# Turned scores in a ring of four unit places, and the token MLP by halves of the channels

## The chip, the core and the metric

The kernel runs on one core of one Trainium2 chip. The metric is the device time of one execution in microseconds (us). Times are medians of several runs; a profile is one further execution, recorded by the hardware profiler, and its rows are what the working below is made of.

The engines of the core have these names in the profile: PE is the matrix engine, PEld its weight loads, DVE the vector engine, ACT the scalar engine, POOL the general one, SP the engine that here only issues DMAs. An engine works through its own instructions in the order in which they were written. "ACTq" and "SPq" rows are DMA issues.

## The reference, cut to what matters

All data are float32. There are 8 batches, 8 heads, 576 tokens, a head dimension of 64, 512 channels, a token MLP of width 256 and a channel MLP of width 1536.

```python
scores = q @ k.T / 8                                   # per batch and head, 576 x 576
thresh = scores.max(-1) - tau
scores = where(scores >= thresh, scores, -1e9)
attn = exp(scores - scores.max(-1)); attn /= attn.sum(-1) + 1e-9
x = heads_side_by_side(attn @ v)                       # batch x 576 x 512
u = x + (relu(x.T @ w_tok1) @ w_tok2).T                # token MLP, mixes tokens
out = u + relu(u @ w_ch1) @ w_ch2                      # channel MLP, mixes channels
```

## The kernel before, in words

**Units, visits, groups.** Attention is cut into 144 units of 128 rows of queries for two heads (a "pair" of heads). Nine units make a visit (two pairs of one batch; the middle unit, t = 4, is shared by both pairs), two visits make a batch. Units are numbered u = 0 to 143; the first batch is u = 0 to 17. Three units in a row (GU = 3) make a group, so a visit has groups 0, 1 and 2, and in a group the units have places 0, 1 and 2.

**One unit.** `scores` (L290s to L313): PE writes q k into two PSUM tiles (L306, pool of two, so a unit's tiles must be read before the next unit's scores), DVE takes the row maximum (L311), POOL makes a bias (L312). `weigh` (L315): ACT reads the scores (L321) into e, 128 x 1152, and takes the exponential with its row sum (L328). `norm` (L332): DVE takes reciprocals (L335, L336), POOL multiplies (L339).

**Turning e.** The product with v needs e with the keys on the partitions. In the first batch `turn` does that on PE (L357) with copies into a tile eT of a group (L359). In all later batches `turn_blocks` (L361) does it for the unit two before the running one: DVE transposes 32 x 32 blocks of e into a tile T of the group (L369), and after the third unit SP issues 16 DMAs (L378) that put the blocks where they belong in eT. T comes from a pool of two tiles with room for three units each; eT is a single tile. `values` (L395) multiplies eT with v on PE (L413, L418), two units after the group's last turn, and ACT copies the result into xT (L423).

```python
T = Ts[key]          # work.tile([P, 4, GU, NK * 32], tag="T"), one per group, two in turn
for a in range(4):
    for i in range(4):
        nc.sync.dma_start(out=eT[32 * a : 32 * a + 32, :, i, :], in_=T[32 * i : 32 * i + 32, a, :, :])
```

**MLPs as filling.** When a batch's values are done, `push` (L603) queues its token MLP, then its channel MLP, as small steps with costs, in `todo`; `fill` (L590) pops steps between the parts of later units, up to a quota. Old channel-MLP steps that are left over (about 45 us of them) are dealt out one ahead of every token step, and two ahead of the steps whose places `push` gets as `waits`. So the order in which PE works is written by this dealing.

`token_mlp` (L430) for a batch: 5 steps transpose xT on PE (L449), and ACT copies into x_sb (L450); 2 steps `tok1`, each 5 matmuls of 512 columns (L456), with a Relu on ACT into a tile `a` (L458); 8 steps `tok2`, each 2 matmuls of 288 columns (L466) and an addition into xT on DVE (L470). The first batch does this in two halves of the channels already, later batches at full width. A float32 matmul stands in the profile as two rows. tok1, tok2 and the channel MLP (`channel_mlp` L484; L509 with a Relu at L510, L530 with an addition at L542) take turns at two PSUM tiles, tag "mm"; each must be emptied by ACT or DVE before it is filled again.

**Loads.** v of a pair is loaded on SP (`load_v`, L110) into a pool of four tiles: at t = 3 of a visit the first pair of the next visit, at t = 7 its second pair (L730). SP's queue holds, in the order written, these loads, the 16 DMAs of each group, 16 small moves per channel-MLP block (L499) and the stores of the output (L549, L569).

Of the kernel before, what the change touches and what calls it, by code (L numbers as in the profile page):

```python
# [9 lines left out]
F32 = mybir.dt.float32  # L10
# [3 lines left out]
AF = mybir.ActivationFunctionType  # L14
ALU = mybir.AluOpType
AX = mybir.AxisListType

P = 128
# [3 lines left out]
def kernel(  # L22
# [25 lines left out]
    nc = tc.nc  # L48
    B, H, S, D = q.shape
    DM = H * D  # L50
# [3 lines left out]
    NI = 4  # L54
    MAIN = NI * P
    LAST = S - MAIN
    NT = NI + 1
    MT = [P] * NI + [LAST]
    NP = H // 2
    NTK = DTOK // P  # L60
    NCC = DM // P
    NJ = DCH // P
    HS = S // 2
    NK = 2 * S // P
# [3 lines left out]
    const = ctx.enter_context(tc.tile_pool(name="const", bufs=1))  # L68
    ld = ctx.enter_context(tc.tile_pool(name="ld", bufs=2))
    work = ctx.enter_context(tc.tile_pool(name="work", bufs=2))  # L70
# [3 lines left out]


    late = ctx.enter_context(ExitStack())
    ps_3rd = late.enter_context(tc.tile_pool(name="ps_3rd", bufs=1, space=bass.MemoryType.PSUM))
    ps_mm = None

# [2 lines left out]
    pairs = [(b, p) for b in range(B) for p in range(NP)]  # L82
# [27 lines left out]
    def load_v(n):  # L110

        b, p = pairs[n]
        lv = ld.tile([P, NK, D], F32, tag="lv", bufs=4, name=f"lv_{n}")
        nc.sync.dma_start(out=lv, in_=v[b].rearrange("h s d -> (h s) d")[2 * S * p : 2 * S * p + 2 * S, :].rearrange("(c p) d -> p c d", p=P))
        vals[n] = lv

# [14 lines left out]
    w1 = const.tile([P, NT, DTOK], F32, name="w1")  # L131
    w2 = const.tile([P, NTK, S], F32, name="w2")
    wc1 = const.tile([P, NJ, NCC, P], F32, name="wc1")
    wc2 = const.tile([P, NJ, DM], F32, name="wc2")

    x_sb = const.tile([P, NT, DM], F32, name="x_sb")
    nc.gpsimd.memset(x_sb[LAST:P, NI, :], 0.0)
    nc.gpsimd.memset(w1[LAST:P, NI, :], 0.0)

# [111 lines left out]
    def need(i):  # L251

        weight(3 * i + 4 - steps_done)

    load_piece(0)
    load_v(0)
    for i in range(1, NRAW):
        load_piece(i)
    load_v(1)


# [14 lines left out]
    st = {}  # L276
    xTs = {}
    eTs = {}
    Ts = {}

    def in_blocks(b):
        return b > 0
# [59 lines left out]
    GU = 3  # L342

    def turn(u, third):

        b, p0, t = units[u]
        key, place = (b, p0, t // GU), t % GU
        e = st[u]

        if third == 0 and place == 0:  # L350
            eTs[key] = work.tile([P, NK, GU * P], F32, tag="T", name=f"eT_{u}")
        if third == 2:
            st.pop(u)
        ps = ps_tr.tile([P, MAIN], F32, tag="tr", name=f"tr{third}_{u}")[:, 0 : 3 * P].rearrange("p (c x) -> p c x", c=3)
        for c in range(3):
            k0 = (3 * third + c) * P
            nc.tensor.transpose(out=ps[:, c, :], in_=e[:, k0 : k0 + P], identity=ident)  # L357
        on = nc.scalar.copy if third == 1 else nc.vector.tensor_copy
        on(out=eTs[key][:, 3 * third : 3 * third + 3, P * place : P * place + P], in_=ps)  # L359

    def turn_blocks(u):  # L361

        b, p0, t = units[u]
        key, place = (b, p0, t // GU), t % GU
        e = st.pop(u)
        if place == 0:
            Ts[key] = work.tile([P, 4, GU, NK * 32], F32, tag="T", name=f"T_{u}")
        T = Ts[key]
        nc.vector.transpose(  # L369
            out=T[:, :, place, :].rearrange("p a (c x) -> p c a x", c=NK), in_=e.rearrange("p (c a x) -> p c a x", c=NK, a=4)  # L370
        )
        if place == GU - 1:
            del Ts[key]
            eT = work.tile([P, GU, 4, NK * 32], F32, tag="eT", bufs=1, name=f"eT_{u}")
            eTs[key] = eT.rearrange("p n i (c x) -> p (n i) c x", c=NK)
            for a in range(4):
                for i in range(4):
                    nc.sync.dma_start(out=eT[32 * a : 32 * a + 32, :, i, :], in_=T[32 * i : 32 * i + 32, a, :, :])  # L378

    def split_middle(n):  # L380

# [8 lines left out]
    copies = deque()  # L390
# [34 lines left out]
                copies.append(lambda x=x, ps=ps: nc.vector.tensor_copy(out=x, in_=ps))  # L425


    hidden = {}

    def token_mlp(b, ps=range(NP)):  # L430

        xT = xTs[b]
        o = S * (b % 2)
        L = len(ps)
        cols = slice(P * ps[0], P * ps[0] + P * L)
        if b not in hidden:
            hidden[b] = work.tile([P, NTK, DM], F32, tag="a", bufs=1, name=f"a_{b}")
        a = hidden[b]

        def psum(name):  # L440
            return (ps_mm or ps_tr).tile([P, DM], F32, tag="mm" if ps_mm else "tr", name=name)

        def turn_x(t, n):
            M = MT[t]
            to = ps_tr.tile([P, MAIN], F32, tag="tr", name=f"tx_{b}_{t}_{ps[0]}")[0:M, 0 : n * L * P].rearrange("p (t c x) -> p t c x", t=n, c=L)
            for i in range(n):
                for c in range(L):
                    tok = o + (t + i) * P
                    nc.tensor.transpose(out=to[:, i, c, :], in_=xT[:, ps[c], tok : tok + M], identity=ident)  # L449
            nc.scalar.copy(out=x_sb[0:M, t : t + n, cols], in_=to.rearrange("q t p d -> q t (p d)"))  # L450

        def tok1(m):
            need(2)
            to = psum(f"t1_{b}_{m}_{ps[0]}")[:, 0 : P * L]
            for t in range(NT):
                nc.tensor.matmul(to, lhsT=w1[:, t, P * m : P * m + P], rhs=x_sb[:, t, cols], start=(t == 0), stop=(t == NT - 1))  # L456
            if ps_mm:
                nc.scalar.activation(out=a[:, m, cols], in_=to, func=AF.Relu)  # L458
            else:
                copies.append(lambda: nc.vector.tensor_scalar(out=a[:, m, cols], in0=to, scalar1=0.0, scalar2=None, op0=ALU.max))  # L460

        def tok2(c, f):
            need(6)
            to = psum(f"t2_{b}_{c}_{f}")[:, 0:HS]
            for m in range(NTK):
                nc.tensor.matmul(  # L466
                    to, lhsT=a[:, m, P * c : P * c + P], rhs=w2[:, m, HS * f : HS * f + HS], start=(m == 0), stop=(m == NTK - 1)
                )
            u = xT[:, c, o + HS * f : o + HS * f + HS]
            nc.vector.tensor_add(out=u, in0=u, in1=to)  # L470

        n = NI // L
        steps = [(0.11 * n * L, lambda t=t: turn_x(t, n)) for t in range(0, NI, n)] + [(0.11 * L, lambda: turn_x(NI, 1))]
        first = len(steps)
        steps += [(1.1 * L, lambda m=m: tok1(m)) for m in range(NTK)]
        steps += [(0.97, lambda c=c, f=f: tok2(c, f)) for c in ps for f in range(2)]
        return steps, (first, first + NTK)

# [120 lines left out]
    early = deque()  # L601

    def push(b):  # L603
        nonlocal quota
        uT = xTs[b]
        steps, waits = token_mlp(b) if b else token_mlp(b, range(NP // 2, NP))
        old = list(todo)
        todo.clear()
        todo.extend(early)
        early.clear()  # L610

        for i, step in enumerate(steps):
            n = 2 if i in waits else 1
            todo.extend(old[:n] + [step])
            del old[:n]
        todo.extend(old)
        for i in range(2) if b % 2 == 0 else range(2, (2 * S + GR - 1) // GR):
            todo.extend(channel_mlp(b - b % 2, uT, i))
        quota = (sum(c for c, _ in todo) - (KEEP if b else KEEP_FIRST)) / (UB - 1)
# [28 lines left out]
    for u in range(len(units) + LAG + 4):  # L648
        on = u < len(units)
        if u == UB:  # L650
            late.close()
            ps_mm = ctx.enter_context(tc.tile_pool(name="ps_mm", bufs=2, space=bass.MemoryType.PSUM))
        if on:
            b_now, p0, t = units[u]
            n = b_now * NP + p0
        w = u - LAG
        back = 0 <= w < len(units)
# [26 lines left out]
        while copies:  # L684
            copies.popleft()()
        if last and u < UB:
            early.extend(token_mlp(0, range(NP // 2))[0])
        elif last:
            push(0)
        if back:  # L690
# [11 lines left out]
        if back and in_blocks(wb):  # L702
            turn_blocks(w)
# [15 lines left out]
        if on:  # L719


            when = {3: (2, 0, 2), 4: (2, 2, 4), 5: (2, 4, 6), 6: (2, 6, 8), 8: (3, 0, 3), 0: (1, 3, 6), 1: (1, 6, 8)}
            if u == 0:
                load_qk(1, (nc.sync, nc.sync), range(0, 3))
            if t in when:
                m, lo, hi = when[t]
                if n + m < len(pairs):
                    load_qk(n + m, (nc.scalar if b_now else nc.sync,) * 2, range(lo, hi))
            if t in (3, 7) and n + 2 + t // 4 < len(pairs):
                load_v(n + 2 + t // 4)  # L730
            if t == 2:
                prep(n + 1)
            if t == 7 and n + 2 < len(pairs):
                prep(n + 2)
# [36 lines left out]
```

## Time and profile before

| what | value |
|---|---|
| median of 3 runs | 1352.67 us (1351.88 to 1352.94) |
| span of the profiled execution, first to last instruction | 1349.9 us |
| PE busy | 1306.6 us, 97% of the span |
| DVE busy | 592.2 us, 44% |
| ACT busy | 585.1 us, 43% |
| POOL busy | 352.5 us, 26% |
| DMA, mean rate | 100 GB/s |
| block transposes on DVE (L369) | 126 of 1364 ns |
| DMAs from T to eT (L378) | 672 of 108 KB, median 2.3 us from issue to landing |

The time that the profiled execution has outside its span isn't in the profile; its span is 2.8 us less than the median of the runs. A row of instruction groups gives line, engine, operation, tiles, shape and count, then after the bar busy time in us, mean ns of one, and the engine's idle time before them with what ended it. A timeline row gives start and length in us, and in brackets the idle time before it and what ended it. "PEclk" is the share of PE's full clock that was granted.

### The profile page before, as it was taken

How to read it: one execution, taken by the hardware profiler on the slowest of the kernel's cores; microseconds unless marked ns; L12 is line 12 of the kernel's file. 1: busy time of each engine (PE TensorE's matmuls, PEld its weight loads, DVE VectorE, ACT ScalarE, POOL GpSimd, SP SyncE). 2: the span in 40 equal slices, each digit the busy share in tenths (PEclk: the TensorE clock that was granted, in tenths of full speed). 3: DMA queues.
4: the chain of work that ended last, by engine and by line, in shares of the span. 5: the costliest groups of instructions: out<-in, count | busy, mean ns of one | idle time of the engine just before them, and what ended most of it. 6: DMA issues, size and time to landing. Idle time of an engine off the chain costs nothing.

```text
span 1349.9 us, 17890 instructions
## 1 busy us (share of the span) xinstructions
PE 1306.6 (97%) x6186; PEld 817.1 (61%) x6186; DVE 592.2 (44%) x1026; ACT 585.1 (43%) x1299; POOL 352.5 (26%) x683
## 2 busy tenths in 40 slices
PE   7888899999999999999999999999999999999999
PEld 5565556547474666655665567565656566575677
DVE  6878874445443435434334445434443454201000
ACT  6777654444445435443434444354333454120110
POOL 4565652222222213222222222222221222100000
PEclk8998999999999999999999999999999999999999
DMA  5535764535353544543345435535443453400000
GB/s 123 120 87 127 199 168 97 127 94 136 83 133 89 114 109 96 126 109 88 86 107 125 98 85 123 125 82 115 109 102 83 114 118 79 112 22 17 23 24 32
DMA packets 296746, 135.31 MB, mean 100 GB/s; under 512 B 204816, under 2 KB 289552, under 8 KB 296656
## 3 DMA queue, kind: packets, MB, share of 16 engines
q1 hardware_dynamic: 168944, 118.27, 34.4%
q10 hardware_dynamic: 127712, 15.90, 7.4%
q8 instruction: 49, 0.80, 0.3%
q14 instruction: 41, 0.34, 0.1%
HBM read 43.25 MB, written 9.44 MB: 39 GB/s over the span
## 4 chain that ended last, share of the span: by engine, by line
PE 86%; DVE 6%; DMA 3%; ACT 2%; SPq 1%; issue 1%; POOL 1%; ACTq 0%; DVEq 0%; POOLq 0%
PE c L530 26%; PE c L509 26%; PE sc L306 11%; PE pv L418 9%; PE t L456 5%; PE t L466 4%; PE pv L413 3%; DVE mx L311 2%; PE tx L449 1%; DMA lk<-in_k_dram 1%; ACT e L321 1%; SPq L378 1%; PE c_h L557 1%; DVE T L369 1%; DVE high L211 1%
## 5 line engine op out<-in xcount | busy, mean ns | idle before, releaser
L509 PE MATMUL c<-xT,wc 128*128 128x256 f32 (+1 forms) x1920 | 400.1, 362 | 0.1
L311 DVE TENSOR_REDUCE mx<-sc 128x1 f32<-128x576 f32 x288 | 204.4, 750 | 444.3 <-PE sc L306 443.2
L530 PE MATMUL c<-wc,g 128*128 128x512 f32 x840 | 379.0, 597 | 0.0
L509 PEld LDWEIGHTS c<-xT,wc 128*128 128x128 f32 x1920 | 334.9, 191 | 69.3 <-issue 29.7
L312 POOL TENSOR_SCALAR bias<-mx,toff 128x1 f32<-128x1 f32 x288 | 81.1, 282 | 775.6 <-DVE mx L311 722.7
L321 ACT ACTIVATE e<-sc,bias 128x576 f32<-128x576 f32 x288 | 199.8, 739 | 182.5 <-POOL bias L312 176.7
L530 PEld LDWEIGHTS c<-wc,g 128*128 128x128 f32 x840 | 154.7, 190 | 176.1 <-issue 172.4
L328 ACT ACTIVATE e<-e,ntau 128x576 f32<-128x576 f32 x288 | 221.1, 771 | 0.0
L339 POOL TENSOR_SCALAR e<-e,rr 128x576 f32<-128x576 f32 x288 | 214.3, 756 | 14.8 <-ACT g L510 2.6
L510 ACT ACTIVATE g<-c 128x256 f32<-128x256 f32 (+1 forms) x240 | 86.7, 361 | 296.5 <-PE c L509 283.4
L306 PE MATMUL sc<-kT,qT 64*128 64x288 f32 (+1 forms) x1280 | 190.3, 433 | 6.9 <-ACT e L321 5.9
L369 DVE STREAM_TRANSPOSE T<-e 128x1152 f32<-128x1152 f32 x126 | 171.9, 1364 | 5.5 <-DMA eT<-T 2.9
L306 PEld LDWEIGHTS sc<-kT,qT 64*128 64x128 f32 (+1 forms) x1280 | 105.2, 178 | 92.2 <-issue 57.2
L418 PE MATMUL pv<-eT,lv 128*64 128x384 f32 (+1 forms) x1024 | 136.8, 408 | 0.0
L418 PEld LDWEIGHTS pv<-eT,lv 128*64 128x64 f32 x1024 | 76.9, 138 | 49.9 <-issue 42.1
L423 ACT COPY xT<-pv 128x384 f32<-128x384 f32 (+1 forms) x56 | 21.0, 400 | 164.6 <-PE pv L418 159.5
L466 PE MATMUL t<-w,a 128*128 128x288 f32 x256 | 75.2, 421 | 8.2 <-DVE xT L470 4.8
L542 DVE TENSOR_TENSOR us<-c,ut 128x512 f32<-128x512 f32 x26 | 17.9, 690 | 137.5 <-PE c L530 122.7
L456 PE MATMUL t<-x_sb,w 128*128 128x512 f32 (+1 forms) x180 | 72.4, 549 | 0.0
L466 PEld LDWEIGHTS t<-w,a 128*128 128x128 f32 x256 | 45.9, 192 | 30.2 <-issue 10.5
L470 DVE TENSOR_TENSOR xT<-xT,t 128x288 f32<-128x288 f32 x64 | 28.3, 446 | 70.6 <-PE t L466 69.9
L328 ACT ACTIVATION_READ_ACCUMULATOR e<-e,ntau 128x1 f32 x288 | 56.7, 197 | 0.0
(51 smaller groups left out, 571.2 us busy)
## 6 DMA issues: line engine op xcount, KB each, us to landing
eT<-T SPq DMA_DIRECT2D x672, 108.0 KB, 2.3
scratch<-in_moe_w_ch_dram SPq DMA_DIRECT2D x24, 512.0 KB, 3.7
lv<-in_v_dram SPq DMA_DIRECT2D x32, 288.0 KB, 3.5
out_dram<-us SPq DMA_DIRECT2D x35, 256.0 KB, 2.2
lk<-in_k_dram ACTq DMA_DIRECT2D x109, 72.0 KB, 2.7
lq<-in_q_dram ACTq DMA_DIRECT2D x106, 72.0 KB, 2.3
ut<-us SPq DMA_DIRECT2D x192, 32.0 KB, 1.9
lk<-in_k_dram SPq DMA_DIRECT2D x19, 72.0 KB, 3.2
```

The lines of the kernel that those rows point to most:

```text
L306: nc.tensor.matmul(sc[h][rows, f, 0:HS], lhsT=qT[r, cols], rhs=kT[r, HS * f : HS * f + HS], start=True, stop=True)
L311: nc.vector.tensor_reduce(out=mx[:, c], in_=sc[h][:, :, 0:HS], axis=AX.XY, op=ALU.max)
L321: nc.scalar.activation(out=eh, in_=sc[h][:, :, 0:HS], func=AF.Prelu, bias=bias[:, h : h + 1], scale=SCALE, alpha=STEEP)
L328: nc.scalar.activation(out=eh, in_=eh, func=AF.Exp, bias=ntau, accum_out=rs[:, h : h + 1])
L339: nc.gpsimd.tensor_scalar(out=eh, in0=eh, scalar1=rr[:, h : h + 1], scalar2=1.0, op0=ALU.mult, op1=ALU.mult)
L369: nc.vector.transpose(out=T[:, :, place, :].rearrange("p a (c x) -> p c a x", c=NK), in_=e.rearrange("p (c a x) -> p c a x", c=NK, a=4))
L418: nc.tensor.matmul(to[r], lhsT=lv[:, j, :], rhs=e[j], start=False, stop=(c == NI - 1), skip_group_check=True)
L456: nc.tensor.matmul(to, lhsT=w1[:, t, P * m : P * m + P], rhs=x_sb[:, t, cols], start=(t == 0), stop=(t == NT - 1))
L466: nc.tensor.matmul(to, lhsT=a[:, m, P * c : P * c + P], rhs=w2[:, m, HS * f : HS * f + HS], start=(m == 0), stop=(m == NTK - 1))
L509: nc.tensor.matmul(ps, lhsT=wc1[:, j, c, :], rhs=uT[:, c, GR * i : GR * i + n], start=(c == 0), stop=(c == NCC - 1))
L510: nc.scalar.activation(out=s["g"][:, j, 0:n], in_=ps, func=AF.Relu)
L530: nc.tensor.matmul(flat, lhsT=s["g"][:, j, P * t : P * t + P], rhs=wc2[:, j, :], start=(j == 0 and b > 0), stop=(j == NJ - 1), skip_group_ ...
```

## The change

The tile T becomes one ring of four unit places (GU + 1). Groups with an even number fill places 0, 1, 2 and groups with an odd number fill 3, 2, 1; so the first unit of a group goes into the one place that the group before it did not use, and the second and third go into places that the group before it did use. The DMAs read the places in the order of the units. The ring's memory is taken when the first batch is over; until then a pool `first` holds there one of the two eT tiles of the first batch, and the other is the eT tile that later batches use.

The token MLP is cut into two halves of the channels for every batch. x_sb and `a` are half as wide, one of each, and used by both halves in turn. `token_steps` writes the new order: turns, tok1 of the first half; turns of the second half; tok2 of the first half; tok1, tok2 of the second half. That makes 18 steps in place of 15 and three places with two old steps ahead in place of two. v has three tiles in place of four: at t = 2 of a visit its own second pair is loaded, at t = 5 the first pair of the next visit.

```diff
+    first = late.enter_context(tc.tile_pool(name="first", bufs=1))
-        lv = ld.tile([P, NK, D], F32, tag="lv", bufs=4, name=f"lv_{n}")
+        lv = ld.tile([P, NK, D], F32, tag="lv", bufs=3, name=f"lv_{n}")
-    x_sb = const.tile([P, NT, DM], F32, name="x_sb")
+    x_sb = const.tile([P, NT, DM // 2], F32, name="x_sb")
...
-            eTs[key] = work.tile([P, NK, GU * P], F32, tag="T", name=f"eT_{u}")
+            odd = (u // GU) % 2
+            pool = work if odd else first
+            eTs[key] = pool.tile([P, NK, GU * P], F32, tag="eT", bufs=1, name=f"eT_{u}")
...
-        if place == 0:
-            Ts[key] = work.tile([P, 4, GU, NK * 32], F32, tag="T", name=f"T_{u}")
-        T = Ts[key]
+        back = (u // GU) % 2
+        slot = GU - place if back else place
         nc.vector.transpose(
-            out=T[:, :, place, :].rearrange("p a (c x) -> p c a x", c=NK), ...
+            out=T[:, slot].rearrange("p a (c x) -> p c a x", c=NK), ...
...
+            slots = slice(GU, 0, -1) if back else slice(0, GU)
-                    nc.sync.dma_start(..., in_=T[32 * i : 32 * i + 32, a, :, :])
+                    nc.sync.dma_start(..., in_=T[32 * i : 32 * i + 32, slots, a, :])
...
-        if b not in hidden:
-            hidden[b] = work.tile([P, NTK, DM], F32, tag="a", bufs=1, name=f"a_{b}")
-        a = hidden[b]
+        xs = slice(0, P * L)
+        a = work.tile([P, NTK, P * L], F32, tag="a", bufs=1, name=f"a_{b}_{ps[0]}")
...
+    def token_steps(b):
+        half = NP // 2
+        ta, ma, sa = token_mlp(b, range(half))
+        tb, mb, sb = token_mlp(b, range(half, NP))
+        n = len(ta) + NTK + len(tb)
+        return ta + ma + tb + sa + mb + sb, (len(ta), n, n + len(sa) + NTK)
...
-        steps, waits = token_mlp(b) if b else token_mlp(b, range(NP // 2, NP))
+        if b:
+            steps, waits = token_steps(b)
+        else:
+            turns, t1, t2 = token_mlp(b, range(NP // 2, NP))
+            steps, waits = turns + t1 + t2, (len(turns), len(turns) + NTK)
...
         if u == UB:
             late.close()
+            ring = ctx.enter_context(tc.tile_pool(name="ring", bufs=1))
+            T = ring.tile([P, GU + 1, 4, NK * 32], F32, name="T")
...
-            if t in (3, 7) and n + 2 + t // 4 < len(pairs):
-                load_v(n + 2 + t // 4)
+            if t in (2, 5) and 1 < n + 1 + t // 3 < len(pairs):
+                load_v(n + 1 + t // 3)
```

More of the change, by code (lines that the diff above doesn't have):

```diff
@@ L76 @@
     late = ctx.enter_context(ExitStack())
+    first = late.enter_context(tc.tile_pool(name="first", bufs=1))
+    T = None
     ps_3rd = late.enter_context(tc.tile_pool(name="ps_3rd", bufs=1, space=bass.MemoryType.PSUM))
@@ L278 @@
     eTs = {}
-    Ts = {}
     def in_blocks(b):
@@ L365, in turn_blocks @@
         e = st.pop(u)
-        if place == 0:
-            Ts[key] = work.tile([P, 4, GU, NK * 32], F32, tag="T", name=f"T_{u}")
-        T = Ts[key]
+        back = (u // GU) % 2
+        slot = GU - place if back else place
         nc.vector.transpose(
-            out=T[:, :, place, :].rearrange("p a (c x) -> p c a x", c=NK), in_=e.rearrange("p (c a x) -> p c a x", c=NK, a=4)
+            out=T[:, slot].rearrange("p a (c x) -> p c a x", c=NK), in_=e.rearrange("p (c a x) -> p c a x", c=NK, a=4)
         )
         if place == GU - 1:
-            del Ts[key]
             eT = work.tile([P, GU, 4, NK * 32], F32, tag="eT", bufs=1, name=f"eT_{u}")
             eTs[key] = eT.rearrange("p n i (c x) -> p (n i) c x", c=NK)
+            slots = slice(GU, 0, -1) if back else slice(0, GU)
             for a in range(4):
                 for i in range(4):
-                    nc.sync.dma_start(out=eT[32 * a : 32 * a + 32, :, i, :], in_=T[32 * i : 32 * i + 32, a, :, :])
+                    nc.sync.dma_start(out=eT[32 * a : 32 * a + 32, :, i, :], in_=T[32 * i : 32 * i + 32, slots, a, :])
     def split_middle(n):
@@ L425, in values @@
                 copies.append(lambda x=x, ps=ps: nc.vector.tensor_copy(out=x, in_=ps))
-    hidden = {}
     def token_mlp(b, ps=range(NP)):
@@ L434, in token_mlp @@
         L = len(ps)
-        cols = slice(P * ps[0], P * ps[0] + P * L)
-        if b not in hidden:
-            hidden[b] = work.tile([P, NTK, DM], F32, tag="a", bufs=1, name=f"a_{b}")
-        a = hidden[b]
+        xs = slice(0, P * L)
+        a = work.tile([P, NTK, P * L], F32, tag="a", bufs=1, name=f"a_{b}_{ps[0]}")
         def psum(name):
@@ L449, in turn_x @@
                     nc.tensor.transpose(out=to[:, i, c, :], in_=xT[:, ps[c], tok : tok + M], identity=ident)
-            nc.scalar.copy(out=x_sb[0:M, t : t + n, cols], in_=to.rearrange("q t p d -> q t (p d)"))
+            nc.scalar.copy(out=x_sb[0:M, t : t + n, xs], in_=to.rearrange("q t p d -> q t (p d)"))
         def tok1(m):
@@ L455, in tok1 @@
             for t in range(NT):
-                nc.tensor.matmul(to, lhsT=w1[:, t, P * m : P * m + P], rhs=x_sb[:, t, cols], start=(t == 0), stop=(t == NT - 1))
+                nc.tensor.matmul(to, lhsT=w1[:, t, P * m : P * m + P], rhs=x_sb[:, t, xs], start=(t == 0), stop=(t == NT - 1))
             if ps_mm:
-                nc.scalar.activation(out=a[:, m, cols], in_=to, func=AF.Relu)
+                nc.scalar.activation(out=a[:, m, :], in_=to, func=AF.Relu)
             else:
-                copies.append(lambda: nc.vector.tensor_scalar(out=a[:, m, cols], in0=to, scalar1=0.0, scalar2=None, op0=ALU.max))
+                copies.append(lambda: nc.vector.tensor_scalar(out=a[:, m, :], in0=to, scalar1=0.0, scalar2=None, op0=ALU.max))
         def tok2(c, f):
@@ L466, in tok2 @@
                 nc.tensor.matmul(
-                    to, lhsT=a[:, m, P * c : P * c + P], rhs=w2[:, m, HS * f : HS * f + HS], start=(m == 0), stop=(m == NTK - 1)
+                    to, lhsT=a[:, m, P * (c - ps[0]) : P * (c - ps[0]) + P], rhs=w2[:, m, HS * f : HS * f + HS], start=(m == 0), stop=(m == NTK - 1)
                 )
@@ L472, in token_mlp @@
         n = NI // L
[L473 to L477, printed above, removed]
+        turns = [(0.11 * n * L, lambda t=t: turn_x(t, n)) for t in range(0, NI, n)] + [(0.11 * L, lambda: turn_x(NI, 1))]
+        return turns, [(1.1 * L, lambda m=m: tok1(m)) for m in range(NTK)], [(0.97, lambda c=c, f=f: tok2(c, f)) for c in ps for f in range(2)]
+    def token_steps(b):
[4 more added lines that the diff above has]
+        return ta + ma + tb + sa + mb + sb, (len(ta), n, n + len(sa) + NTK)
     moves = deque()
@@ L686 @@
         if last and u < UB:
-            early.extend(token_mlp(0, range(NP // 2))[0])
+            early.extend(sum(token_mlp(0, range(NP // 2)), []))
         elif last:
```

## The prediction

> **What bounds the kernel now.** I read the page first, for the busy shares and the chain, then what PE waits for, then the timeline around single units.
>
> ```profile
> span 1349.9 us, 17890 instructions
> PE 1306.6 (97%) x6186; PEld 817.1 (61%) x6186; DVE 592.2 (44%) x1026; ACT 585.1 (43%) x1299; POOL 352.5 (26%) x683
> PE 86%; DVE 6%; DMA 3%; ACT 2%; SPq 1%; issue 1%; POOL 1%; ACTq 0%; DVEq 0%; POOLq 0%
> ```
>
> PE is busy for 97% of the span and carries 86% of the chain that ended last. By stretches (the windows view) its idle time lies before 310 us and in the last stores; from 310 to 1242 us it is 4.4 us. So there is little to gain: work taken off DVE, ACT or SP gives nothing, and whatever makes PE wait is added in full. What PE waits for in the token MLP, the part that the change rearranges:
>
> ```profile
> PE t L466 <- DVE xT L470: 4.8, 3, 3.0
> PE t L466 <- ACT g L510: 3.2, 3, 1.6
> PE tx L449 <- ACT x_sb L450: 1.7, 3, 1.2
> ```
>
> The columns are total us, times, longest. Together 9.7 us; without the 3.0 in the first batch, 6.7.
>
> **The ring's wait.** In the built program of the changed kernel, the second turn of every group (place 1) waits for all 16 DMAs of the group before; the first and third turn wait for none. Before, the first turn of a group waited for the DMAs of the group two back. So the DMAs had four units, and now have two. The worst group shows how to read it:
>
> ```profile
> 834.99 11.57 SPq L378 DMA_DIRECT2D eT<-T  x16
> 843.09 1.36 DVE L369 STREAM_TRANSPOSE T<-e 128x1152 f32<-128x1152 f32 x1
> 853.99 1.42 DVE L311 TENSOR_REDUCE mx<-sc 128x1 f32<-128x576 f32 x2 [9.54 <-PE sc L306]
> ```
>
> SP needs 11.57 us to issue the 16 DMAs; the last lands at 849.1, some 2.5 us after the row's end. The place-1 turn of the next group ran at 843.09, so it would have waited 6.0 us. I did this for all 41 pairs of groups: in 22 the landing is after the turn's start, 51 us in all, 2.3 each. But DVE's next work, the maximum, waits for PE: here DVE was idle for 9.54 us, and in all 41 cases the idle time up to the next maximum is longer than the wait. With landings 3 us later still, 0.1 us in all would reach a maximum; 4 us later, 5; 6 us later, 38. So DVE's idle time is the cover, and the wait costs PE nothing by way of the scores. The turn's other customers have time too: the third turn comes a unit later, e has three tiles.
>
> The cover is gone where an addition of tok2 (L470) stands between that turn and the next maximum: DVE is in order, the addition waits with the turn, its PSUM tile isn't emptied, and the tok2 two tiles later waits on PE. Before, 6 of the place-1 turns have such an addition behind them; in the changed program's order 10 (one of them in the first group, which waits for no DMA, so nine count). Two of these have a late landing in the trace and only short work on PE behind. Unit 99:
>
> ```profile
> 758.37 12.37 SPq L378 DMA_DIRECT2D eT<-T  x16
> 767.06 1.24 PE L306 MATMUL sc<-kT,qT 64*128 64x288 f32 x8
> 769.95 1.36 DVE L369 STREAM_TRANSPOSE T<-e 128x1152 f32<-128x1152 f32 x1
> 771.11 1.24 PE L466 MATMUL t<-w,a 128*128 128x288 f32 x4 [0.82 <-ACT g L510]
> ```
>
> The landing is at 772.4. In the new order PE runs scores, tok2, ch1, tok2, ch1, tok2 there. Additions take 0.45 (L470), a tok2 0.97 (4 rows 0.243 apart), a short ch1 0.9. The first addition ends at 770.4; the turn waits until 772.5 and ends at 773.9; the second addition ends at 774.3, and the third tok2, ready at 772.3, starts then: 2.0 us lost. The same in unit 135 (landing 1088.8, turn at 1086.7, one ch1 more ahead of it): 1.3. The other seven land early or have values (2 to 4 us of PE) behind them. I take **+3.3 us**; bounds 0 (the turns shift out of the way) and 9 x 2.3 = +21.
>
> **tok1 at half width.** Two rows of the profile:
>
> ```profile
> L456 PE MATMUL t<-x_sb,w 128*128 128x512 f32 x140 | 62.8, 595 | 0.0
> L456 PE MATMUL t<-x_sb,w 128*128 128x256 f32 x40 | 9.6, 387 | 0.0
> ```
>
> Mean lengths overlap, so the distance of starts counts: 0.429 at 512 columns, 0.216 at 256 (medians of these rows in the trace). Seven batches: 280 x 0.216 - 140 x 0.429 = 60.5 - 60.1 = **+0.4 us**. The 256-column weight load, 0.19, stays below 0.216. [...]
>
> **The new order of steps.** The transposes stay 20 per batch. ACT gets one x_sb copy and two Relus more per batch, under 1 us of an engine that is 43% busy. 18 steps with 3 double places want 21 old steps ahead, against 17. Batches 3 and 5 run out, and three tok2 stand in a row right behind scores (units 84 and 120). Two PSUM tiles and an addition that comes after a maximum (1.42), the reciprocals (0.33) and, in unit 84, the turn (1.36): From the start of scores: two tok2 end at 2.2 and 3.2, the reciprocals at 3.05, the first addition at 3.5, so the third tok2 waits 0.35 in both units; in unit 84 the turn then runs to 4.9, the second addition to 5.35, and the ch1 that wants its tile waits 0.9. **+1.6 us**; bounds 0 and 2 x 3.0, the longest of the first row above. In batch 7, after the last unit, two tok2 stand together; a free DVE empties their tiles in time: 0.
>
> **tok2 behind ACT.** The 3.2 us come in batches 2, 4 and 6, where two short ch1 and then a tok2 follow scores: the tile that tok2 wants is emptied by a Relu which stands on ACT behind L321. The new order has four such places instead of three (both halves of batch 2, second halves of 4 and 6). At 1.1 each, **+1.1 us**; bounds -3.2 (all gone) and twice in each of six batches, 12 x 1.1 - 3.2 = +10.
>
> **At nothing.** DMAs from T: the same 672, 108 KB each; packets in the trace are already 1152 bytes, one unit's piece. Places in descending order have no row; between 2.3 (eT<-T) and 3.2 us (lk<-in_k on SP, 32-number pieces) to landing I take 2.3; 0.9 more would add 0.9 in units 99 and 135, 1.8. The issue rows (0.6 us for eT<-T, 0.5 for lk and lv) leave SP's load as it is. v: the tile taken at t = 2 was last read a visit earlier at the end of t = 0, the one at t = 5 at the end of t = 3, so SP, behind which the 16 moves and the next group's DMAs queue, shouldn't be held; a v load lands in 3.5 us and is wanted two units later. A late one would hold values: at most the 1.8 of the longest such wait in the trace, per visit. The first group of batch 1 now waits for the eT tile of batch 0, read long before. DVE's turns write another stride, same shape: 1364 ns.
>
> **Sum.** 0.4 + 3.3 + 1.6 + 1.1 = 6.4 us on the profiled execution's 1349.9 us of span, what lies outside unchanged. The span is 2.8 below the median of the runs; put on the median, 1352.7 + 6.4 = **1359 us**.
>
> **The rivals.** *Hidden anyway:* the turns and additions fall otherwise than in this trace, and only the certain 0.4 and a wait or two are left: within 2.7 us of before, 1354. For it: in the order of before, a wait would reach an addition behind 3 of the 41 turns only; against it: PE has no idle time to swallow the rest. *Faster:* tok2 of the first half now separates tok1 from the place where PE waited. If all 6.7 us of waits go and the ring's wait stays in DVE's idle time, 1352.7 - 6.7 + 0.4 = 1346. It decides only if ACT's Relu is ahead of L321 in every second half; in the written order it isn't. *Much slower:* landings come 3 us later, as SP lags (the issue at 834.99 above began 3.6 us after its turn's end), and all nine turns with additions behind them hold PE, 2.3 + 3 less some 2 of cover, 3.3 each: 30 us for 3.3 of mine, and gaps past 3 us slow the clock as well:
>
> ```profile
> 111.00:115.00 4.00, 3.72 (x13) 1.98 (x15) 2.94 (x5) 4.00 (x10) 2.69 (x3) 0.50 0.04 7
> 180.00:186.00 6.00, 5.06 (x45) 3.27 (x43) 2.44 (x4) 2.59 (x5) 2.52 (x3) 1.00 0.66 169
> ```
>
> The column after the counts of POOL is the granted clock: 0.50 for 4 us after PE's wait of 4.37 us, 1.00 around one of 1.82. With one such gap, 2 us, the time is 1352.7 + 6.4 + 26.7 + 2 = 1388. It decides from landings about 2 us later on. *The change isn't what it says:* had the ring been tracked as one tile, the first turn would wait a unit after the issue; the built program shows that it doesn't.
>
> **How the numbers follow.** My sum, slower by 2.7 to 13 us: 0.60. Hidden anyway: 0.22. Faster: 0.08. Much slower: 0.10. A measurement of this kernel tells 0.2%, 2.7 us, from no change. So faster 0.08, same 0.22, slower 0.70. The range leaves out most of faster and of much slower: 1351 to 1367.
>
> **What would show it.** Right: idle time of DVE before the turn's line put down to DMA eT<-T, some 50 us in place of 2.9, at every third turn; PE's waits for additions (tok2 or ch1 behind DVE xT) up by 4 to 6 us, in units 84, 99 and 135; tok1 some 280 rows of 256 columns, no busier. Wrong: PE waiting at scores behind L321, values waiting for eT or lv, or the chain's PE share falling while DVE's DMA wait stays small.

## The result, and the profile after

The changed kernel takes 1360.76 us (median of 4 runs, 1359.34 to 1364.26), the kernel before beside it 1352.81 (4 runs). The ratio is 1.0063, 95% interval [1.0048, 1.0077]: slower by 6.5 to 10.4 us. The prediction was 1359.0 us, slower by 6.4. The profiled execution of the changed kernel took 1361.66 us. From its page, the span, the engines and the shares of the chain that ended last:

```profile
span 1359.8 us, 18192 instructions
...
PE 1311.4 (96%) x6326; PEld 842.7 (62%) x6326; DVE 592.7 (44%) x1026; ACT 587.5 (43%) x1320; POOL 352.7 (26%) x683
...
PE 85%; DVE 6%; DMA 2%; ACT 2%; POOL 1%; issue 1%; SPq 1%; ACTq 0%; DVEq 0%; POOLq 0%
```

The span is 9.9 us longer. PE is busy 4.8 us longer and idle 5.1 us longer, so about half of the loss is waiting, and half is PE being busy longer. The waits of the changed kernel (total us, times, longest):

```profile
DVE us L497 <- DMA out_dram<-us: 37.1, 10, 8.7
DVE T L371 <- DMA eT<-T: 28.7, 13, 4.6
...
PE t L465 <- DVE xT L469: 5.7, 5, 2.8
...
PE c L513 <- DVE xT L469: 5.2, 3, 4.3
...
PE tx L448 <- ACT x_sb L449: 2.3, 2, 2.1
...
PE t L465 <- ACT g L514: 1.1, 3, 0.4
...
PE c L513 <- ACT g L514: 0.9, 1, 0.9
```

The second row is the ring's wait, 28.7 us of DVE in place of 2.9. PE's waits for additions (`DVE xT`) grew from 4.8 to 10.9 us; of the 6.1 us, 4.3 are one wait of a ch1 matmul (`c L513`). The first row is an old wait: DVE turns xT into the tile `us` and must wait until a store has read it. Before it was nearly as large:

```profile
DVE us L493 <- DMA out_dram<-us: 31.3, 11, 8.4
```

Two groups of the page after, the turn and tok1:

```profile
L371 DVE STREAM_TRANSPOSE T<-e 128x1152 f32<-128x1152 f32 x126 | 171.9, 1365 | 52.3 <-DMA eT<-T 28.7
...
L455 PE MATMUL t<-x_sb,w 128*128 128x256 f32 x320 | 75.2, 382 | 0.5 <-ACT x_sb L449 0.4
```

The turn costs DVE what it did (1365 ns), but the engine stands 52.3 us before it in place of 5.5. tok1 has 320 rows of 256 columns.

**Where the 9.9 us come from.** I took from both traces the start of each unit's first maximum (L311, L312 after), which follows the scores on PE, and read how far the changed kernel lags behind at the end of each batch's units. The growth of the lag, per 18 units:

| units | growth, us | what stands there after |
|---|---|---|
| 0 to 17, 18 to 35 | +0.65, -0.16 | start; two profiles of one kernel (without the ring, below) are 1.3 us apart by 290 us |
| 36 to 53 | +1.14 | a wait of 2.09 for x_sb, and a granted clock of 0.50 behind it |
| 54 to 71 | -0.80 | tok2 waits less behind ACT's Relu |
| 72 to 89 | +1.28 | unit 84, three tok2 in a row |
| 90 to 107 | **+6.79** | units 98 and 99 |
| 108 to 125 | +0.94 | unit 120, three tok2 in a row |
| 126 to 143 | +0.06 | unit 135 |

Two thirds of the loss are one place. DVE there in the changed kernel (timeline: start, length, in brackets the idle time before and what ended it):

```profile
758.39 1.36 DVE L371 STREAM_TRANSPOSE T<-e 128x1152 f32<-128x1152 f32 x1
761.71 0.69 DVE L546 TENSOR_TENSOR us<-c,ut 128x512 f32<-128x512 f32 x1 [1.96 <-PE c L534]
...
765.24 1.36 DVE L371 STREAM_TRANSPOSE T<-e 128x1152 f32<-128x1152 f32 x1
775.29 0.71 DVE L497 STREAM_TRANSPOSE us<-xT 128x512 f32<-128x512 f32 x1 [8.69 <-DMA out_dram<-us]
775.93 1.38 DVE L312 TENSOR_REDUCE mx<-sc 128x1 f32<-128x576 f32 x2
...
777.50 0.43 DVE L469 TENSOR_TENSOR xT<-xT,t 128x288 f32<-128x288 f32 x1
777.85 1.37 DVE L371 STREAM_TRANSPOSE T<-e 128x1152 f32<-128x1152 f32 x1
779.15 0.41 DVE L469 TENSOR_TENSOR xT<-xT,t 128x288 f32<-128x288 f32 x1
```

SP's queue in the same stretch:

```profile
759.82 13.06 SPq L380 DMA_DIRECT2D eT<-T  x16
772.98 0.53 SPq L553 DMA_DIRECT2D out_dram<-us  x1
```

And PE:

```profile
769.95 1.24 PE L465 MATMUL t<-w,a 128*128 128x288 f32 x4
771.02 1.05 PE L513 MATMUL c<-xT,wc 128*128 128x128 f32 x8
772.44 1.24 PE L465 MATMUL t<-w,a 128*128 128x288 f32 x4 [0.37 <-ACT g L514]
777.99 2.08 PE L513 MATMUL c<-xT,wc 128*128 128x128 f32 x8 [4.31 <-DVE xT L469]
779.86 2.13 PE L465 MATMUL t<-w,a 128*128 128x288 f32 x4
```

Read them backwards. PE's ch1 at 777.99 waits 4.31 us for the addition of 777.50. That addition isn't held by the ring: the place-1 turn comes behind it (777.85), with no idle time before it. It is late because DVE stood 8.69 us at the transposition into `us`, a single tile that still had to be stored. The store was issued at 772.98, since SP had the group's 16 DMAs to issue first (13.06 us), because the addition that fills `us` (761.71) now comes behind the group's last turn (758.39). Before, the two were the other way round:

```profile
756.33 0.69 DVE L542 TENSOR_TENSOR us<-c,ut 128x512 f32<-128x512 f32 x1 [1.08 <-PE c L530]
756.93 1.37 DVE L369 STREAM_TRANSPOSE T<-e 128x1152 f32<-128x1152 f32 x1
...
771.23 0.67 DVE L493 STREAM_TRANSPOSE us<-xT 128x512 f32<-128x512 f32 x1
```

```profile
757.05 0.34 SPq L549 DMA_DIRECT2D out_dram<-us  x1
758.37 12.37 SPq L378 DMA_DIRECT2D eT<-T  x16
```

The store went out 1.3 us ahead of the 16, and the next block's transposition (771.23, with no wait) came a unit later than after. Both moves come from the dealing of the new token steps: they put the last step of one channel-MLP block later, from ahead of tok1 to behind it, and the second step of the next block a unit earlier. The third double place has no part in this: the run without it, further down, keeps this order (turn 758.96, addition into `us` 762.28 in its trace).

The wait is paid twice. Windows of the changed kernel; the column after the busy times is the granted clock:

```profile
774.00:778.00 4.00, 0.01 (x1) 0.01 (x1) 2.67 (x7) 0.96 (x2) 0.78 (x3) 0.64 0.22 77
778.00:782.00 4.00, 4.00 (x14) 3.43 (x15) 1.56 (x2) 2.23 (x6) 1.21 (x2) 0.50 0.10 26
782.00:790.00 8.00, 7.93 (x70) 6.28 (x70) 2.89 (x7) 1.23 (x5) 1.14 (x3) 1.00 0.25 47
```

From 778 to 782 us the granted clock was 0.50: the eight ch1 matmuls took 2.08 in place of 1.05, the tok2 2.13 in place of 1.14. That is 2.0 us. With 0.5 of other waits (0.92 + 0.37 behind ACT's Relu, in place of 0.82 before), 4.31 + 2.0 make the 6.79.

### The profile page after: what moved, and what is told of

The parts are those of the page before. It is cut to its first block, busy times and chain, and to the rows that moved or that the text cites. A ratio compares the mean times of both kernels' runs of the same rounds, so it can differ in the third digit from the quotient of the medians.

```text
span 1359.8 us, 18192 instructions
## 1 busy us (share of the span) xinstructions
PE 1311.4 (96%) x6326; PEld 842.7 (62%) x6326; DVE 592.7 (44%) x1026; ACT 587.5 (43%) x1320; POOL 352.7 (26%) x683
## 4 chain that ended last, share of the span: by engine, by line
PE 85%; DVE 6%; DMA 2%; ACT 2%; POOL 1%; issue 1%; SPq 1%; ACTq 0%; DVEq 0%; POOLq 0%
PE c L534 26%; PE c L513 26%; PE sc L307 11%; PE pv L420 8%; PE t L455 5%; PE t L465 4%; PE pv L415 3%; DVE mx L312 2%; PE tx L448 1%; ACT e L322 1%; SPq L380 1%; PE tr L360 1%; DVE wc L215 1%; PE c_h L561 1%; DMA lq<-in_q_dram 1%
## 5 line engine op out<-in xcount | busy, mean ns | idle before, releaser
L513 PE MATMUL c<-xT,wc 128*128 128x256 f32 (+1 forms) x1920 | 401.2, 363 | 6.2 <-DVE xT L469 5.2
L513 PEld LDWEIGHTS c<-xT,wc 128*128 128x128 f32 x1920 | 335.2, 191 | 70.3 <-issue 22.3
L312 DVE TENSOR_REDUCE mx<-sc 128x1 f32<-128x576 f32 x288 | 204.1, 749 | 394.4 <-PE sc L307 393.1
L322 ACT ACTIVATE e<-sc,bias 128x576 f32<-128x576 f32 x288 | 199.6, 740 | 195.4 <-POOL bias L313 191.7
L371 DVE STREAM_TRANSPOSE T<-e 128x1152 f32<-128x1152 f32 x126 | 171.9, 1365 | 52.3 <-DMA eT<-T 28.7
L455 PE MATMUL t<-x_sb,w 128*128 128x256 f32 x320 | 75.2, 382 | 0.5 <-ACT x_sb L449 0.4
L455 PEld LDWEIGHTS t<-x_sb,w 128*128 128x128 f32 x320 | 59.5, 190 | 16.3 <-issue 6.1
```

Of the source, the lines that this page charges most:

```text
L312: nc.vector.tensor_reduce(out=mx[:, c], in_=sc[h][:, :, 0:HS], axis=AX.XY, op=ALU.max)
L322: nc.scalar.activation(out=eh, in_=sc[h][:, :, 0:HS], func=AF.Prelu, bias=bias[:, h : h + 1], scale=SCALE, alpha=STEEP)
L371: nc.vector.transpose(out=T[:, slot].rearrange("p a (c x) -> p c a x", c=NK), in_=e.rearrange("p (c a x) -> p c a x", c=NK, a=4))
L513: nc.tensor.matmul(ps, lhsT=wc1[:, j, c, :], rhs=uT[:, c, GR * i : GR * i + n], start=(c == 0), stop=(c == NCC - 1))
```

## The experiments

**The theories.** A: the large loss is the store behind the 16 DMAs, from the new order of token steps; the ring and v cost next to nothing. B: the prediction's, that the ring's wait holds additions. C: all three parts lose a little. Each ratio below is against the kernel before on the same chip.

**The ring alone.** The diff's lines on T, `first` and `ring`; token MLP and v as before.

> The kernel before with the ring of four unit places alone (and the eT tile of the first batch in its memory); token MLP at full width, four tiles of v. Theory A (the loss of unit 99 comes from the store that stands behind a group's 16 DMAs in SP's queue, which only the new order of the token steps brings about): DVE's idle time before the turns rises by some 45 us, put down to the DMAs from T, but PE loses at most 1 us: 1352 to 1354 us. Theory B (the prediction's: the ring's wait holds tok2's additions): the kernel loses 3 us or more, 1356 us. Theory C (all three parts lose a little each): about 1355 us.

Measured: 1352.02 us (12 runs), ratio 1.0000 [0.9991, 1.0009]. The ring's wait is there in full:

```profile
L371 DVE STREAM_TRANSPOSE T<-e 128x1152 f32<-128x1152 f32 x126 | 172.0, 1366 | 56.4 <-DMA eT<-T 32.4
```

So DVE's idle time hides it wherever the scores are next, as the prediction said, and in the order of before it reaches nothing else. B falls as the cause of the large loss.

**The halves alone.** The diff's lines on `x_sb`, `a`, `token_mlp` and `token_steps`; T and v as before.

> The kernel before with the token MLP by halves of the channels alone (half-wide x_sb and a, the new order of steps); two tiles T, four tiles of v. Theory A: nearly the whole loss, 1359 to 1361 us, with PE waiting some 4 us in unit 99 and DVE's us transpose waiting over 8 us for a store there. Theory B: 1355 to 1356 us, the part of the prediction's sum that is not the ring's. Theory C: about 1355 us.

Measured: 1361.3 us (5 runs), ratio 1.0069 [1.0057, 1.0082]: the whole loss, with PE's wait of 4.32 us at 778.0 of its trace.

**v alone.** `bufs=3` and the loads at t = 2 and 5.

> The kernel before with three tiles of v and the new times of its loads alone. Theories A and B: no change, 1352 to 1354 us. Theory C: up to 1355 us, with values waiting for v or SP held at a load.

Measured: 1351.4 us (12 runs), ratio 0.9998 [0.9989, 1.0007]. The ring alone and v alone cost nothing that these runs resolve, so C falls.

**A second tile `us`.** The changed kernel and one edit:

```diff
-                s["us"] = work.tile([P, GR // P, 4, NCC * 32], F32, tag="us", bufs=1, name=f"us_{b}_{i}")
+                s["us"] = work.tile([P, GR // P, 4, NCC * 32], F32, tag="us", bufs=2, name=f"us_{b}_{i}")
```

> The changed kernel with two tiles us in place of one (4 KB of the memory that the change frees), so that the transpose of us no longer waits for the store of the block before. Theory A: the loss of unit 99 goes, about 6.8 us: 1354 us (1352.5 to 1355.5). Theory B: the turn's wait stays, so does the loss: 1360 to 1361 us. Theory C: 1358 to 1361 us.

Measured: 1355.79 us (7 runs), ratio 1.0031 [1.0018, 1.0043]. DVE in the same place:

```profile
759.44 0.69 DVE L546 TENSOR_TENSOR us<-c,ut 128x512 f32<-128x512 f32 x1 [1.97 <-PE c L534]
...
764.25 0.67 DVE L497 STREAM_TRANSPOSE us<-xT 128x512 f32<-128x512 f32 x1
...
769.39 0.43 DVE L469 TENSOR_TENSOR xT<-xT,t 128x288 f32<-128x288 f32 x1
772.56 1.38 DVE L371 STREAM_TRANSPOSE T<-e 128x1152 f32<-128x1152 f32 x1 [2.73 <-DMA eT<-T]
773.86 0.78 DVE L469 TENSOR_TENSOR xT<-xT,t 128x288 f32<-128x288 f32 x2
```

The transposition (764.25) waits for nothing, and 90 to 107 lose 1.6 us in place of 6.8. The time is 0.3 us above A's range, since 1.6 us of that place stay. Now what the prediction described comes to light: the turn waits 2.73 us for the ring, two additions stand behind it, and PE's ch1 waits 0.72 (2.0 predicted).

**The same cure without a second tile.** The transposition into the single `us` is written four steps later:

```diff
-            if j == 1:
+            if j == 5:
                 s["us"] = work.tile(...)
```

> The changed kernel with its single tile us, but the transposition into us is written four channel-MLP steps later (after the sixth step of the block, not the second). Theory A (that transposition waited 8.7 us for a store behind 16 DMAs in SP's queue and held DVE in unit 99): in its new place the store is out within 1 us, so the gain is that of a second tile: 1355 to 1357 us. Rival (the second tile helped in another way than by this one wait): 1360.8, as the changed kernel.

Measured: 1356.27 us (6 runs), ratio 1.0026 [1.0015, 1.0037]. In its trace:

```profile
775.13 1.38 DVE L371 STREAM_TRANSPOSE T<-e 128x1152 f32<-128x1152 f32 x1 [2.71 <-DMA eT<-T]
776.43 0.42 DVE L469 TENSOR_TENSOR xT<-xT,t 128x288 f32<-128x288 f32 x1
776.77 0.69 DVE L497 STREAM_TRANSPOSE us<-xT 128x512 f32<-128x512 f32 x1
```

The transposition (776.77) finds its tile free. Two independent edits that take away this one wait give back the same 4 to 5 us.

**A control of the second tile.** Full-width token MLP in the order of before, with ring, three buffers of v and two tiles `us`.

> The token MLP at full width as before, with the ring, three buffers of v and two tiles us. A control of the second tile us, and the ring and v together. Theory A: in the order of before no transposition waits long for us, so the second tile gains nothing: 1352.0 us, as before (1351 to 1353). Rival: the second tile us helps at all the blocks, whatever the order, and what it gained beside the changed kernel (5 us) is no sign of one place: 1347.

Measured: 1353.09 us (12 runs), ratio 1.0004 [0.9995, 1.0013]. Taking away all of the `us` wait, 31.3 us in the order of before, gains nothing: there, it was hidden everywhere. So the wait isn't what costs; its place is. No combination here beats the kernel before.

**The ring beside the halves.** The halves with three buffers of v and two tiles `us`, without the ring; then this pair (without and with ring) once more, side by side on one chip.

> The halves and the three buffers of v, with two tiles us and the two tiles T of before, so no ring. It is the run with two tiles us (1355.8 us) less the ring. Theory A (the store behind the 16 DMAs, through the single us, was the large loss; the ring's wait costs only what PE waits in unit 99 for the second addition, 0.7 us): 1355.0 us, unit 99 without the wait for the addition. Theory B (the ring's wait holds additions as the prediction priced it, 2.0 in unit 99 and 1.3 in unit 135): 1352.5. If the ring costs nothing at all: 1355.8.

> The same kernel as halves_us2, beside after_us2_b on one chip, for the size of the ring's share beside the halves. Its time is the base for the other: 1353.7 us, and PE doesn't wait for a Relu in units 63 and 135.

> The same kernel as after_us2: halves_us2_b plus the ring. Theory A by the traces (the ring's wait sends the third tok2 in units 63 and 135 to the PSUM tile that a Relu empties: 0.37 of waiting and 0.26 of longer rows each, and nothing net in unit 99): 1.3 us more than the base, 1355.0. Theory B (the prediction's ring term): 3.3 more, 1357.0. If the difference between the two runs before was chance: the same as the base.

| | without the ring | with it |
|---|---|---|
| first time | 1353.71, 1.0009 [1.0000, 1.0017] | 1355.79, 1.0031 [1.0018, 1.0043] |
| side by side | 1354.71, 1.0014 [1.0002, 1.0027] | 1356.52, 1.0028 [1.0016, 1.0041] |

By the ratios the ring costs 0.0022 and 0.0014 of the time, some 3 and 2 us, where it costs 0.0000 alone. The first time, the interval without the ring (1352.3 to 1354.6 us) holds B's 1352.5 and not A's 1355.0, but its two runs were on two chips. Side by side, the two means differ by 1.9 us, and the scatter of the 11 and 7 runs leaves some 2 us either way. The traces show 1.3, the same in both pairs, and not in unit 99, where A had put 0.7. In unit 63, first without the ring and then with it, PE's third tok2:

```profile
452.73 1.05 PE L511 MATMUL c<-xT,wc 128*128 128x128 f32 x8
453.62 1.14 PE L463 MATMUL t<-w,a 128*128 128x288 f32 x4
```

```profile
453.33 1.05 PE L513 MATMUL c<-xT,wc 128*128 128x128 f32 x8
454.75 1.24 PE L465 MATMUL t<-w,a 128*128 128x288 f32 x4 [0.37 <-ACT g L514]
```

and DVE with the ring:

```profile
453.95 1.38 DVE L371 STREAM_TRANSPOSE T<-e 128x1152 f32<-128x1152 f32 x1 [1.82 <-DMA eT<-T]
455.25 0.42 DVE L469 TENSOR_TENSOR xT<-xT,t 128x288 f32<-128x288 f32 x1
```

With the addition behind a waiting turn (455.25), the tile of the tok2 before comes free late. Without the ring, the third tok2 starts (453.62) behind the addition of 452.93 and ahead of ACT's next Relu (453.81), so its PSUM tile is the one that the addition empties. With the ring it starts ahead of the addition and behind the Relu: it has the other of the two tiles. From the start of the ch1 to the start of this tok2, 1.42 us pass in place of 0.89, and the tok2 takes 1.24 in place of 1.14: 0.63 us, and unit 135 has the same wait of 0.37, with the ring only. In unit 99, PE waits twice 0.55 without the ring (first for one addition, then for the next) and 0.37 + 0.72 with it, so nothing net. The side-by-side times exclude neither B's 3.3 us, nor 1.3, nor nothing at all; the traces speak for 1.3.

**Two double places.** The changed kernel with two tiles `us`, and

```diff
-        return ta + ma + tb + sa + mb + sb, (len(ta), n, n + len(sa) + NTK)
+        return ta + ma + tb + sa + mb + sb, (len(ta), n)
```

> The changed kernel with two tiles us and without the third place that gets two old steps, so that in batches 3 and 5 the last tok2 don't stand three in a row behind scores; unit 99 is as in the run with two tiles us (1355.8 us). Theory A (the order's term is PE's waits in units 84 and 120, 1.1 and 0.75 there): 1353.9 us, and those waits gone. Rival (the rest of the loss is spread: narrower matmuls, more instructions): 1355.8, whatever those two units show.

Measured: 1357.14 us (5 runs), ratio 1.0035 [1.0023, 1.0047], no faster than 1.0031: A's 1353.9 missed. The trace says why only in part. Unit 84 with this edit, two tok2 and no wait before a third:

```profile
636.78 2.19 PE L465 MATMUL t<-w,a 128*128 128x288 f32 x8
639.36 2.86 PE L513 MATMUL c<-xT,wc 128*128 128x256 f32 x12 [0.39 <-DVE xT L469]
```

and in the changed kernel:

```profile
634.20 2.21 PE L465 MATMUL t<-w,a 128*128 128x288 f32 x8
637.15 1.24 PE L465 MATMUL t<-w,a 128*128 128x288 f32 x4 [0.75 <-DVE xT L469]
638.78 1.56 PE L513 MATMUL c<-xT,wc 128*128 128x256 f32 x6 [0.39 <-DVE xT L469]
```

The 0.75 is gone in unit 84, and units 72 to 89 lose 0.9 us less. In unit 120 the 0.75 stays: it falls on the ch1 that comes in the place of the third tok2, since two tok2 right behind scores already fill both tiles. And units 90 to 107 lose 0.4 more, with a new wait of 0.45 for an addition at 795 us. Besides, this execution is 3.5 us behind its partner by unit 53, 1.8 of it in one wait for loads of q and k; PE's waits in that batch's token MLP are the same in both. So the parts named give back 0.5 of the 1.9 us expected. From unit 54 on, however, this execution and the one with three double places fall behind by the same 3.7 us in all: no gain of this edit is shown.

## Why the prediction was right, and where it wasn't

The number was right (1359.0 for 1360.76), the sign too, but its largest term had the right place (unit 99) with the wrong cause.

- **The ring's wait, +3.3.** The step that failed. The prediction counted what is queued behind the waiting turn and found units 99 and 135; it said that the turn's wait holds additions there. In unit 99 the additions were held, 4.31 us and not 2.0, but by the transposition into `us`, which the prediction didn't look at: it looked at what stands behind the ring's turn on DVE, and in SP's queue at the loads of v. That the dealing moves the addition that fills `us` behind the turn, and with it the store behind 16 DMAs, is fixed by the order of the program, so it could have been known beforehand. Unit 135 cost 0.55 + 0.37 in waits, but 0.82 had been there before, so the place lost 0.1 in place of 1.3; and the 0.55 is there without the ring too. Alone, the ring costs 0; beside the halves 1.3 by the traces, in units 63 and 135.
- **The slow clock** stood under the rival "much slower", for gaps past 3 us. The trace of before has two of these, 3.02 us (138.41) and 4.37 (111.28), with a granted clock of 0.50 behind each. The change brought one more, the 4.31 us in unit 99, with 0.50 behind it: 2.0 us as priced there, and not from late landings. But in the changed kernel's trace the clock was 0.50 also behind gaps of 2.09 us (290.65) and 1.90 (159.31), and 1.00 behind one of 2.83 (138.71). The prediction's harmless 1.82 is at 159.48 in the trace of before, with 1.00 behind it; the longest wait in the row of 180 to 186 us shown for it is 0.94.
- **DVE's idle time as cover**: right. 28.7 us of `eT<-T` in the row, 47.5 with the waits of the same turns that the trace puts down to other DMAs (lk 9.1, ut 4.9, lq 4.8), of some 50 predicted, and the ring alone at 1.0000.
- **The new order of steps, +1.6**: right in place and nearly in size. Unit 84 waits 0.75 + 0.39 (0.35 + 0.9 predicted), unit 120 0.75 (0.35); the lag grows by 1.28 and 0.94. That another dealing would give these back wasn't confirmed: the run with two double places gained 0.9 in unit 84, nothing in unit 120, and lost 0.4 elsewhere.
- **tok2 behind ACT, +1.1**: wrong sign. The waits for `ACT g` are 2.3 us in place of 3.2 (2.0 in the two rows above, and two of 0.12 that these leave out), and units 54 to 71 are 0.8 faster. There were more such places, as said, but each waits 0.12 to 0.92 and not 1.1. The old 1.58 is gone: in unit 63 ACT now has the Relus of the two ch1 behind scores ahead of L322, which the prediction denied of the written order.
- **tok1, +0.4**: measured +0.9, from 70.4 to 71.3 us of distances between starts without the idle time. The steady distance is 0.216 as expected, against 0.429 at 512 columns before. Some rows next to another operation take 0.1 us more, 20 of them in place of 17, which is 0.3 of the 0.5 left.
- **Units 36 to 53, +1.1**: not foreseen. The first transposes of a half wait 2.09 us for an x_sb copy of ACT's, in place of two waits of 1.24 (for such a copy) and 1.26 (for an addition), and behind it the granted clock was 0.50 (291 to 293 us).
- **At nothing**: v is right (0.9998), DMAs in descending order of places too (the ring alone at 1.0000). The transposition into `us` and the store that it waits for stood in no term.

So the sum came near by luck: a stall that it didn't see (6.8 with the slow clock behind it) took the place of terms that came to little or nothing in the changed kernel (3.3 and 1.1).

## What to carry to other kernels

When an order of steps changes, follow every queue that a moved step writes to, not only the engine that runs it: a store that slips behind a burst of DMA issues keeps its tile for the length of the burst (here 13.06 us of issues on SP), and with a single tile the next writer stops its whole engine (DVE, 8.69 us). A long wait need not cost anything, and a cost needs no new wait: here 31 us of the same wait cost nothing before, and one 8.7 us instance of it, moved a unit, cost 6.8. A part that is free alone needn't be free beside another: the ring cost nothing in the old order and 1.3 us, by the traces, in the new one.

## What the runs showed of the hardware that was not expected

The clock fell behind a gap of 2.1 us in some executions and not in others. Without the ring, the same kernel was profiled twice; in both, PE waited 2.09 us for x_sb and then ran tok2. The windows behind the wait, first and second time:

```profile
291.00:295.00 4.00, 4.00 (x26) 1.70 (x26) 0.45 (x1) 0.62 (x3) 0.00 (x0) 1.00 0.16 24
```

```profile
291.00:295.00 4.00, 4.00 (x13) 2.04 (x13) 0.91 (x2) 1.64 (x5) 0.00 (x0) 0.57 0.25 41
```

The granted clock is 1.00 in the first and 0.57 in the second. From the first tok2 behind the wait to the next scores, PE took 5.4 us and 7.1: 1.6 us of difference. Of the eight profiles with that wait, two kept the clock: from 286 to 296 us it was 1.00 in these and 0.83 in the six others. What surrounds the wait are transposes: in the first profile, 3.4 us pass from the end of the scores (285.8) to tok2 (289.19), in which PE only transposes xT and waits. Whether the transposes matter, and why the same wait kept the clock in two profiles, was not shown: no run here took the transposes away.

A wait in PE's list can cost more than its bracket says. In unit 63, the row of the ch1 (452.73 + 1.05) ends 0.16 us after the next one starts when nothing waits. So the bracket of 0.37, counted from that row's end, stands for a start 0.53 us later, and the tok2 behind it takes 0.10 longer.
